# Chunk 0 of a fused retention and GELU-MLP kernel: two token units multiplied by seven half-size products, and a group of weight sums moved in VectorE's order

## The chip, the core and the metric

The kernel runs on one core of a Trainium2 chip. The core has a matrix engine (TensorE, "PE" in the profile, its weight loads "PEld"), a vector engine (VectorE, "DVE"), an engine for activations (ScalarE, "ACT"), GpSimd ("POOL"), which here issues the loads, and SyncE ("SP"), which issues the stores and the transposing transfers. Each engine takes its instructions in the order of the program and waits on semaphores for the others. The metric is the device time of one execution in microseconds; lower is better.

## What is computed

Eight heads of retention attention, without a softmax, over 8 sequences of 576 tokens, and then an MLP with a sigmoid-approximated GELU over all 4608 tokens:

```python
scores = scale * np.matmul(q, k.transpose(0, 1, 3, 2))
gamma = 1.0 - 2.0 ** (-5.0 - np.arange(H))
Dmat = np.where(rel >= 0, gamma[:, None, None] ** rel, 0.0)
attn_out = np.matmul(scores * Dmat, v)             # [8, 8, 576, 64]
x = attn_out.transpose(0, 2, 1, 3).reshape(4608, 512)
h = x @ w_in                                       # 512 x 2048
g = h * (1.0 / (1.0 + np.exp(-1.702 * h)))
out = g @ w_out                                    # 2048 x 512
```

## The kernel before

**Tiling.** The 4608 tokens are 36 units of 128 tokens (two units of four blocks of 64 for each pair of sequences, and one that joins their tails); four units make a chunk, so there are nine chunks. For each unit the kernel loads K, Q and V (`load`, on POOL's queue), transposes K and Q (`transposes` on PE with copies by DVE and ACT for the early units, `dma_transpose` on SP's queue from unit 8 on), scales V by powers of gamma (`scale_v`, L351, DVE), and then works in blocks of 64 tokens: masked scores inside a block (`scores`, `scores_out`), the running state K^T V (`state_both`, L427, on PE; `state_sum`, L440, on DVE; `state_cast`, L452, on ACT) and the products with both (`inter`, `values`), whose sum is scaled into xT (`x_out_pair`, L548, DVE). `block` strings these together for two units.

**The MLP.** For each of 16 slices f of the hidden width, `up` (L560) makes four matmuls of 128x512 over the chunk's 512 tokens and ACT's Gelu writes gT. The second product, g @ w_out, is made in one of two ways. `down` (L588) is the plain one: for one unit r and a group s of four slices, four matmuls of 128x512, 16 for a unit; `finish_unit` copies the bank out by ACT and stores it. `Pair` (L637) takes two groups of tokens at once by the Strassen-Winograd scheme: gT and w_out are each split in two along the hidden width (even and odd slices), tokens in two rows, the output in two column halves; instead of eight half-size products there are seven, with sums made beforehand and afterwards. The sums of gT are made by `Pair.sums` (L650): three additions into `gsum` and two subtractions in place. The sums of w_out are made once by `wsums` (L622), five operations for each of the four loaded groups of w_out. `Pair.run` (L696) makes the seven products in PSUM banks a and b by turns; three quarters are copied out by ACT (`copy`), six combinations go to DVE (`comb`). Between the products it calls `hook(i)`, where the caller puts other work. In `product` a matmul names the sum that it reads, so it waits for that one alone: `wsummed(n)` gives sum n of slices 2k and 2k+1 under the key of group k // 2.

**Order.** `Program.op` appends each operation to its engine's list in the order in which the Python code calls it, and derives waits from keys that it reads and writes. Nothing is reordered afterwards: an operation that waits holds up all that follows it on its engine.

**The stage of the change.** `lead_in` (L819) does units 0 to 7 up to their transposes and chunk 0's MLP. After `up(0, f)` for f = 8 to 15 (L912) come the second products of chunk 0, all by `down`: units 0 and 1 by turns (banks A and B) through s = 0 to 3, then unit 2, then unit 3. After each `down` of unit 1 a group of w_out sums is made. Six pieces of work for units 4 to 7 are put between the `down` calls, by the dictionary `work` with (unit, group) as key: the transposes and V scalings of units 4, 5, 6, 7, the scores and states of units 4 and 5 (`ahead45`), and their block (`block(2, ...)`). At (1, 3) the scaling of V of unit 4 and its transposes are called ahead of the last `wsums`. In chunks 1 to 7 (`steady`) all second products are made by `Pair(0, 2, 2)`, in chunk 8 units 3 and 0 by `Pair(3, 0, 1)` and units 1 and 2 by `down`.

**Banks.** PSUM banks C, D serve scores, K, E states, X, Y the block outputs, A and B the MLP; the transposes of early units borrow C, D, E, K and B. `turn()` gives A and B alternately.

Of the kernel before, what the change touches and what calls it, by code (L numbers as in the profile page):

```python
# [160 lines left out]
def bass_retnet_parallel__then__act_gelu_quick_kernel(  # L161
# [10 lines left out]
    with es:  # L172
# [160 lines left out]
        def gq_next(t):  # L333
            dst, src = gq[:, t, :, :], gq[:, 0, :, :]
            if t == 4:
                for i in range(2):
                    op("dve", lambda e, i=i: e.tensor_tensor(
                        gq[:, 4, :, 64 * i : 64 * i + 64], gq[:, 0, :, 0:64],
                        gpow[:, 4, :, None].to_broadcast([P, 4, 64]), ALU.mult),
                       reads=[f"gq{a}_0" for a in range(4)] + ["gpow4"], writes=[f"gq{a}_4" for a in range(4)])  # L340
                return
            if t == 5:
                op("dve", lambda e: e.tensor_copy(dst, src),
                   reads=[f"gq{a}_0" for a in range(4)], writes=[f"gq{a}_5" for a in range(4)])
                return
            op("dve", lambda e: e.tensor_tensor(
                dst, src, gpow[:, t, :, None].to_broadcast([P, 4, P]), ALU.mult),
               reads=[f"gq{a}_0" for a in range(4)] + [f"gpow{t}"], writes=[f"gq{a}_{t}" for a in range(4)])
# [211 lines left out]
        def up(c, f, lo=0, hi=4, b=None):  # L560
            b = b or "AB"[f % 2]
            n0, n1 = P * lo, P * hi
            for a in range(4):
                op("pe", lambda e, a=a: e.matmul(  # L564
                    bank[b][:, n0:n1], w_in_sb[:, a, P * f : P * f + P], xT[c % 2][:, a, n0:n1],
                    start=(a == 0), stop=(a == 3)),
                   reads=[f"win{f}"] + [f"x{c % 2}_{j}_{hh}" for j in range(lo, hi) for hh in range(2)],
                   writes=[b])
            op("act", lambda e: e.activation(  # L569
                gT[:, f, n0:n1], bank[b][:, n0:n1], AF.Gelu_apprx_sigmoid),  # L570
               reads=[b], writes=[f"g_{f}_{j}" for j in range(lo, hi)])
# [16 lines left out]
        def down(c, r, s, b, n0=0, n1=DM):  # L588
            for f in range(4 * s, 4 * s + 4):
                op("pe", lambda e, f=f: e.matmul(  # L590
                    bank[b][:, 0 : n1 - n0], gT[:, f, P * r : P * r + P], w_out_sb[:, f, n0:n1],
                    start=(f == 0), stop=(f == NF - 1)),
                   reads=[f"g_{f}_{r}", f"wout{f // 4}"], writes=[b])
# [42 lines left out]

        class Pair:  # L637

            def __init__(self, r0, r1, nt):
                self.r, self.nt, self.n = (r0, r1), nt, P * nt  # L640

            def gpart(self, row, col, f0, f1):
                t0 = P * self.r[row]
# [6 lines left out]
            def sums(self, f0, f1):  # L650
                a, g = (lambda r, c: self.gpart(r, c, f0, f1)), (lambda r, c: self.gkeys(r, c, f0, f1))
                for n, x, y in ((1, (1, 0), (1, 1)), (2, (0, 0), (0, 1)), (0, (0, 0), (1, 1))):
                    op("dve", lambda e, n=n, x=x, y=y: e.tensor_tensor(  # L653
                        gsum[:, n, f0 // 2 : f1 // 2, 0 : self.n], a(*x), a(*y), ALU.add),
                       reads=g(*x) + g(*y), writes=[f"gs{n}_{k}" for k in range(f0 // 2, f1 // 2)])
                for x, y in (((1, 0), (0, 0)), ((0, 1), (1, 1))):
                    op("dve", lambda e, x=x, y=y: e.tensor_tensor(a(*x), a(*x), a(*y), ALU.subtract),  # L657
                       reads=g(*x) + g(*y), writes=g(*x))
# [5 lines left out]
                return f  # L664

            def summed(self, n):
                return lambda k, t: (gsum[:, n, k, P * t : P * t + P], f"gs{n}_{k}")

            def product(self, b, left, right, more=False, late=0):

# [14 lines left out]
                return bank[b][:, 0 : 256 * self.nt].rearrange("p (t n) -> p t n", t=self.nt), [b]  # L685

            def tmp(self):
                return wtmp[:, 0 : 256 * self.nt].rearrange("p (t n) -> p t n", t=self.nt), ["wtmp"]

            def copy(self, dst, src):  # L690
                op("act", lambda e: e.activation(dst[0], src[0], AF.Copy), reads=src[1], writes=dst[1])  # L691
# [127 lines left out]
        def lead_in():  # L819
            load_kq0(0)  # L820
            load_kq0(1)
            iota_small()
            iota_large()
            load_v(0)
            load(1)
            load(2)
            load_win(0, 2)
            load_win(2, 2)
            load(3)
            load_win(4, 2)  # L830
            load_win(6, 2)
            load_win(8, 4)
            load_win(12, 4)
            for i in range(4):
                load_wout(i)
            for u in range(4, NPE + 4):
                load(u)
            op("dve", lambda e: e.memset(warmt.ap(), 0.0), writes=["warm"])
            warm_quads(NQUAD)
            warm(44, "A", 64)  # L840
            setup_dve()
            setup_dve2()
            setup_vfac()
            for a in range(4):
                gq_first(a)
            g_powers()
            gelu_table()
            cast_kq0(0, "dve")
            transpose_pe(0, 0, "E")
            transpose_copy(0, 0, "E", "dve")  # L850
            cast_kq0(1, "dve")
            warm(4)
            transpose_pe(0, 1, "B")
            transpose_copy(0, 1, "B", "dve")
            scale_v(0)
            warm(2)
            scores(0)
            scores_out(0, 1, 0)
            scores_out(0, 1, 1)
            warm(1, "A", 256)  # L860
            state_half(0, 0)
            transpose_pe(1, 0, "E")
            transpose_copy(1, 0, "E", "act")
            transpose_pe(1, 1, "B")
            transpose_copy(1, 1, "B", "act")
            scale_v(1)
            block1(0)
            warm(1, "A", 256)
            scores(1)
            scores_out(1, 1, 0)  # L870
            scores_out(1, 1, 1)
            gq_next(1)
            warm(1)
            state_half(1, 0)
            transpose_pe(2, 0, "E")
            transpose_copy(2, 0, "E", "act")
            warm(1)
            block1(1)
            transpose_pe(2, 1, "B")
            transpose_copy(2, 1, "B", "act")  # L880
            warm(2)
            scores(2)
            scale_v(2)
            scores_out(2, 1, 0)
            scores_out(2, 1, 1)
            up_group(0, 0, 2, 0, 2, "A")
            state_half(2, 0)
            up_group(0, 2, 2, 0, 2, "B")
            gq_next(2)
            block1(2)  # L890
            transpose_pe(3, 0, "E")
            transpose_copy(3, 0, "E", "dve")
            transpose_pe(3, 1, "D")
            transpose_copy(3, 1, "D", "act")
            up_group(0, 0, 4, 2, 3, "A")
            scale_v(3)
            scores(3)
            scores_out(3, 1, 0)
            scores_out(3, 1, 1)
            gq_next(3)  # L900
            warm(1, "E", 256)
            state_half(3, 0)
            up_group(0, 4, 2, 0, 2, "B")
            block1(3)
            up_group(0, 4, 2, 2, 3, "A")
            up_group(0, 6, 2, 0, 2, "B")
            up_group(0, 0, 4, 3, 4, "C")
            up_group(0, 4, 2, 3, 4, "A")
            up_group(0, 6, 2, 2, 4, "B")
            gq_next(4)  # L910
            gq_next(5)
            for f in range(8, NF):  # L912
                up(0, f)
            def ahead45():
                ahead(2)
                for u in (4, 5):
                    state_sum(u, 0)
                    state_sum(u, 1)
                state_cast(4, 6)
                scores_out(4, 2, 0)  # L920
                scores_out(4, 2, 1)

            work = {
                (1, 3): lambda: (scale_v(4), transposes(4, "E", "D", "dve")),
                (2, 0): lambda: (transposes(5, "E", "D", "dve"), scale_v(5)),
                (2, 1): ahead45,
                (3, 1): lambda: now(block(2, lambda: None)),
                (3, 2): lambda: (transposes(6, "C", "D", "dve"), scale_v(6)),
                (3, 3): lambda: (transposes(7, "E", "K", "dve"), scale_v(7)),
            }  # L930
            for r, s in [(i % 2, i // 2) for i in range(8)] + [(i // 4, i % 4) for i in range(8, NF)]:
                down(0, r, s, "AB"[r % 2])
                if (r, s) in work:
                    work[r, s]()
                if r == 1:
                    wsums(s)
                if s == 3:
                    finish_unit(0, r, "AB"[r % 2])

        def steady():  # L940
            four = Pair(0, 2, 2)
# [146 lines left out]
```

## Time and profile before

| | us |
|---|---|
| runs shown | 288.30, 289.47, 290.53 (median 289.47) |
| profiled execution | 289.72 |
| its span, first to last instruction | 287.9 |
| PE busy | 279.0 |
| DVE busy | 181.5 |
| ACT busy | 130.1 |
| POOL busy | 110.1 |

The mean granted clock of PE over the span is 0.994 of full speed. The chain that ended last is 82% PE, 7% POOL, 6% DMA and 3% DVE.

The profile is one execution. Times in it are microseconds from the start of the span. "L590" is line 590 of the kernel above. An instruction's row gives start, duration, engine, line, operation, the tile that it writes and those that it reads, their shapes, and in brackets how long the engine stood idle before it and which instruction of another engine released it. Rows of pipelined engines overlap a little, so a row of several (x5) is shorter than the sum of single durations.

### The profile page before, as it was taken

To read this page: it belongs to the slowest core of one execution; us is meant where nothing else is said; L and a number is where in the kernel's file an instruction comes from. 1 tells how busy PE (TensorE), PEld (TensorE's weight loads), DVE (VectorE), ACT (ScalarE), POOL (GpSimd) and SP (SyncE) were. 2 spreads that over 40 slices of the span, in tenths; PEclk is the share of its full clock that TensorE was granted. 3 is DMA by queue.
4 is the path that set the end of the run, shared out by engine and by line. 5 is a ranking of instruction groups with operands and counts; after the bars stand their busy time and mean duration, and the time that the engine had idled before them with its cause. 6 is when DMAs were issued, how large, how long until landed. Compare 5 with 4: busy or idle time off the path is not lost.

```text
span 287.9 us, 8938 instructions
## 1 busy us (share of the span) xinstructions
PE 279.0 (97%) x4010; PEld 178.7 (62%) x4010; DVE 181.5 (63%) x350; ACT 130.1 (45%) x229; POOL 110.1 (38%) x141
## 2 busy tenths in 40 slices
PE   8999999999879999999999999999999999999996
PEld 6575455888653488348834883488348834883474
DVE  5953667568857967495949593859395928650240
ACT  7456334662117541654175417531754175306611
POOL 9999889000870860068006900670072000000000
PEclk9999999999979999999999999999999999999999
DMA  9999999999999990889398978892896070012012
GB/s 171 180 205 206 202 234 249 235 142 202 101 234 243 104 194 21 229 99 198 68 224 105 171 99 233 111 181 73 227 114 74 13 208 2 2 64 84 0 55 93
DMA packets 116790, 40.69 MB, mean 141 GB/s; under 512 B 104080, under 2 KB 109968, under 8 KB 116752
## 3 DMA queue, kind: packets, MB, share of 16 engines
q0 software_dynamic: 79712, 22.82, 68.7%
q1 hardware_dynamic: 36896, 17.24, 23.0%
q8 instruction: 31, 0.51, 0.7%
q10 hardware_dynamic: 144, 0.07, 0.1%
q14 instruction: 7, 0.06, 0.1%
HBM read 36.70 MB, written 9.44 MB: 160 GB/s over the span
## 4 chain that ended last, share of the span: by engine, by line
PE 82%; POOL 7%; DMA 6%; DVE 3%; ACT 1%; issue 0%; POOLq 0%
PE psA L564 17%; PE psB L564 17%; PE psA L675 16%; PE psB L675 15%; DMA vn<-in_v_dram 6%; POOL w_in_sb L269 3%; PE psB L578 3%; PE psA L578 2%; PE psA L590 2%; PE psB L590 2%; POOL kqn L234 2%; PE psX L489 2%; POOL vn L247 1%; POOL w_out_sb L276 1%; PE psC L505 1%; PE psK L434 1%
## 5 line engine op out<-in xcount | busy, mean ns | idle before, releaser
L234 POOL DMA_DIRECT2D kqn<-in_k_dram x39 | 35.0, 907 | 106.1 <-DMA kqT<-kqn 104.4
L564 PE MATMUL psA<-xT,w_in_sb 128*128 128x512 bf16 x240 | 61.7, 379 | 0.0
L564 PE MATMUL psB<-xT,w_in_sb 128*128 128x512 bf16 x240 | 61.7, 379 | 0.0
L653 DVE TENSOR_TENSOR gsum<-gT 128x1024 bf16<-128x1024 bf16 (+1 forms) x48 | 28.7, 654 | 48.3 <-ACT gT L569 45.6
L569 ACT ACTIVATE gT<-psB 128x512 bf16<-128x512 f32 x60 | 35.8, 597 | 28.6 <-PE psB L564 28.4
L569 ACT ACTIVATE gT<-psA 128x512 bf16<-128x512 f32 x60 | 35.8, 597 | 22.5 <-PE psA L564 22.3
L564 PEld LDWEIGHTS psB<-xT,w_in_sb 128*128 128x128 bf16 x240 | 19.7, 97 | 31.2 <-ACT gT L569 14.2
L564 PEld LDWEIGHTS psA<-xT,w_in_sb 128*128 128x128 bf16 x240 | 19.4, 97 | 30.9 <-ACT gT L569 14.3
L247 POOL DMA_DIRECT2D vn<-in_v_dram x40 | 37.0, 939 | 0.1
L234 POOL DMA_DIRECT2D kqn<-in_q_dram x37 | 33.4, 915 | 0.6 <-issue 0.6
L675 PE MATMUL psA<-wsum,gT 128*128 128x256 bf16 x240 | 29.8, 278 | 0.0
L458 ACT ACTIVATE kv<-stm 128x1024 bf16<-128x1024 f32 (+1 forms) x18 | 15.5, 863 | 29.9 <-DVE stm L449 29.9
L675 PE MATMUL psB<-wsum,gT 128*128 128x256 bf16 x240 | 28.9, 273 | 0.0
L675 PEld LDWEIGHTS psA<-wsum,gT 128*128 128x128 bf16 x240 | 23.6, 100 | 4.2 <-ACT gT L569 1.0
L675 PEld LDWEIGHTS psB<-wsum,gT 128*128 128x128 bf16 x240 | 23.1, 98 | 4.1 <-ACT gT L569 1.5
L353 DVE TENSOR_TENSOR vp<-vn,vfac 128x512 bf16<-128x512 f32 x36 | 23.0, 684 | 3.5 <-DMA vn<-in_v_dram 3.5
L552 DVE TENSOR_TENSOR xT<-psX,gq 128x512 bf16<-128x512 f32 x16 | 11.0, 689 | 18.3 <-PE psX L527 18.3
L657 DVE TENSOR_TENSOR gT<-gT 128x1024 bf16<-128x1024 bf16 (+1 forms) x32 | 19.5, 651 | 0.0
L691 ACT ACTIVATE osb<-psA 128x512 f32<-128x512 f32 (+1 forms) x12 | 7.0, 579 | 23.1 <-PE psA L675 23.1
L691 ACT ACTIVATE osb<-psB 128x512 f32<-128x512 f32 (+1 forms) x12 | 6.7, 562 | 19.1 <-PE psB L675 19.1
L675 PE MATMUL psA<-w_out_sb,gsum 128*128 128x256 bf16 x120 | 14.6, 273 | 0.4 <-issue 0.3
L675 PE MATMUL psB<-w_out_sb,gsum 128*128 128x256 bf16 x120 | 14.4, 273 | 0.0
(108 smaller groups left out, 433.9 us busy)
## 6 DMA issues: line engine op xcount, KB each, us to landing
vn<-in_v_dram POOLq DMA_DIRECT2D x32, 256.0 KB, 4.9
out_dram<-osb SPq DMA_DIRECT2D x31, 256.0 KB, 2.3
kqn<-in_k_dram POOLq DMA_DIRECT2D x31, 128.0 KB, 4.6
kqn<-in_q_dram POOLq DMA_DIRECT2D x31, 128.0 KB, 5.0
w_out_sb<-in_moe_w_out_dram POOLq DMA_DIRECT2D x4, 512.0 KB, 13.4
w_in_sb<-in_moe_w_in_dram POOLq DMA_DIRECT2D x8, 128.0 KB, 5.3
w_in_sb<-in_moe_w_in_dram POOLq DMA_DIRECT2D x4, 256.0 KB, 7.5
vn<-in_v_dram POOLq DMA_DIRECT2D x8, 128.0 KB, 4.2
```

The costliest lines, as they stand in the source:

```text
L234: e.dma_start(kqn[sl][p0 : p0 + n, which, :, :], src[b, :, s0 : s0 + n, :].rearrange("h p d -> p h d"),)
L247: e.dma_start(vn[sl][p0 : p0 + n, :, :], v[b, :, s0 : s0 + n, :].rearrange("h p d -> p h d"))
L353: op(eng, lambda e: e.tensor_tensor(vp[u % NVP].ap(), vn[sl].ap(), vfac[:, ty, :, None].to_broadcast([P, H, DH]), ALU.mult), reads=[f"vn{s ...
L458: op("act", lambda e: e.activation(kv[:, i0 % NKV : i0 % NKV + n, :, :], stm[:, i0 % 8 : i0 % 8 + n, :, :], AF.Copy), reads=[f"stm{(i0 + i ...
L564: op("pe", lambda e, a=a: e.matmul(bank[b][:, n0:n1], w_in_sb[:, a, P * f : P * f + P], xT[c % 2][:, a, n0:n1], start=(a == 0), stop=(a == ...
L569: op("act", lambda e: e.activation(gT[:, f, n0:n1], bank[b][:, n0:n1], AF.Gelu_apprx_sigmoid), reads=[b], writes=[f"g_{f}_{j}" for j in ra ...
L578: op("pe", lambda e, a=a, f=f, i=i: e.matmul(bank[b][:, n * i : n * i + n], w_in_sb[:, a, P * f : P * f + P], xT[c % 2][:, a, P * lo : P * ...
L590: op("pe", lambda e, f=f: e.matmul(bank[b][:, 0 : n1 - n0], gT[:, f, P * r : P * r + P], w_out_sb[:, f, n0:n1], start=(f == 0), stop=(f == ...
L653: op("dve", lambda e, n=n, x=x, y=y: e.tensor_tensor(gsum[:, n, f0 // 2 : f1 // 2, 0 : self.n], a(*x), a(*y), ALU.add), reads=g(*x) + g(*y ...
L657: op("dve", lambda e, x=x, y=y: e.tensor_tensor(a(*x), a(*x), a(*y), ALU.subtract), reads=g(*x) + g(*y), writes=g(*x))
L675: op("pe", lambda e, x=x, y=y, t=t, s=not more and t == 0 and k == 0, z=k == NF // 2 - 1: e.matmul(bank[b][:, 256 * t : 256 * t + 256], x, ...
L691: op("act", lambda e: e.activation(dst[0], src[0], AF.Copy), reads=src[1], writes=dst[1])
```

## The change

Three things are changed.

`Pair` takes a fourth argument `at`, the place in `gsum` and `wtmp` where its sums and its intermediate result lie, and the keys of these become one for each 128 columns.

In chunk 0 units 2 and 3 are multiplied by `Pair(2, 3, 1).run` instead of by eight calls of `down`. Their sums are called in two halves, `sums(0, 8)` ahead of `up(0, 8)` and `sums(8, 16)` after the last `up`, both ahead of the loop that calls `wsums`. The pieces of work that stood after the `down` calls of units 2 and 3 go into the hooks of the run in the same order (hook 0 for (2, 0), and so on to hook 6 for (3, 2)); the piece of (3, 3) follows the run. Units 2 and 3 are then stored in the order 3, 2.

In the loop over units 0 and 1, `wsums(s)` is called ahead of the piece of work and no longer after it. Since only (1, 3) has one there, the last group of w_out sums comes ahead of unit 4's scaling of V and of its transposes' copies.

`Pair.run` calls `turn()` three times, so that banks A and B change places in the chunks that follow.

```diff
-            def __init__(self, r0, r1, nt):
-                self.r, self.nt, self.n = (r0, r1), nt, P * nt
+            def __init__(self, r0, r1, nt, at=0):
+
+                self.r, self.nt, self.n, self.at = (r0, r1), nt, P * nt, P * at
+
+            def places(self):
+                return range(self.at // P, self.at // P + self.nt)
...
-                        gsum[:, n, f0 // 2 : f1 // 2, 0 : self.n], a(*x), a(*y), ALU.add),
-                       reads=g(*x) + g(*y), writes=[f"gs{n}_{k}" for k in range(f0 // 2, f1 // 2)])
+                        gsum[:, n, f0 // 2 : f1 // 2, self.at : self.at + self.n], a(*x), a(*y), ALU.add),
+                       reads=g(*x) + g(*y), writes=[f"gs{n}_{k}_{j}" for j in self.places() for k in range(f0 // 2, f1 // 2)])
...
             def tmp(self):
-                return wtmp[:, 0 : 256 * self.nt].rearrange("p (t n) -> p t n", t=self.nt), ["wtmp"]
+                w = wtmp[:, 2 * self.at : 2 * self.at + 256 * self.nt]
+                return w.rearrange("p (t n) -> p t n", t=self.nt), [f"wtmp{j}" for j in self.places()]
...
             gq_next(4)
             gq_next(5)
+            pair = Pair(2, 3, 1)
+            pair.sums(0, 8)
             for f in range(8, NF):
                 up(0, f)
+            pair.sums(8, 16)
...
-            for r, s in [(i % 2, i // 2) for i in range(8)] + [(i // 4, i % 4) for i in range(8, NF)]:
-                down(0, r, s, "AB"[r % 2])
+            for i in range(8):
+                r, s = i % 2, i // 2
+                down(0, r, s, "AB"[r])
+                if r == 1:
+                    wsums(s)
                 if (r, s) in work:
                     work[r, s]()
-                if r == 1:
-                    wsums(s)
                 if s == 3:
-                    finish_unit(0, r, "AB"[r % 2])
+                    finish_unit(0, r, "AB"[r])
+
+            def hook(i):
+                k = (2 + i // 4, i % 4)
+                if k in work:
+                    work[k]()
+
+            pair.run(0, hook)
+            work[3, 3]()
```

More of the change, by code (lines that the diff above doesn't have):

```diff
@@ L666, in summed @@
             def summed(self, n):
-                return lambda k, t: (gsum[:, n, k, P * t : P * t + P], f"gs{n}_{k}")
+                return lambda k, t: (gsum[:, n, k, self.at + P * t : self.at + P * t + P], f"gs{n}_{k}_{self.at // P + t}")
             def product(self, b, left, right, more=False, late=0):
```

## The prediction

> **What bounds the kernel now.** I read the page first, for the engine that is full and for the clock.
>
> ```profile
> PE 279.0 (97%) x4010; PEld 178.7 (62%) x4010; DVE 181.5 (63%) x350; ACT 130.1 (45%) x229; POOL 110.1 (38%) x141
> ...
> PEclk9999999999979999999999999999999999999999
> ```
>
> TensorE (PE) is busy 279.0 of 287.9 us: fewer columns on it would help, if it is never made to wait instead. One slice has a lower clock. The change lies near 24 to 54 us, so I next listed VectorE (DVE) there in order of time (start, duration, engine, line, operation, count, idle time before it and what ended that).
>
> ```profile
> 22.34 0.97 DVE L343 COPY gq<-gq 128x512 f32<-128x512 f32 x1
> 27.84 1.77 DVE L630 TENSOR_TENSOR wsum<-w_out_sb 128x512 bf16<-128x512 bf16 x5 [4.53 <-DMA w_out_sb<-in_moe_w_out_dram]
> 30.53 1.77 DVE L630 TENSOR_TENSOR wsum<-w_out_sb 128x512 bf16<-128x512 bf16 x5 [0.92 <-DMA w_out_sb<-in_moe_w_out_dram]
> 33.13 1.77 DVE L630 TENSOR_TENSOR wsum<-w_out_sb 128x512 bf16<-128x512 bf16 x5 [0.83 <-DMA w_out_sb<-in_moe_w_out_dram]
> 38.10 0.69 DVE L353 TENSOR_TENSOR vp<-vn,vfac 128x512 bf16<-128x512 f32 x1 [3.21 <-DMA vn<-in_v_dram]
> 38.71 0.42 DVE L385 COPY kqT<-psE 128x512 bf16<-128x512 bf16 x1
> 39.05 1.76 DVE L630 TENSOR_TENSOR wsum<-w_out_sb 128x512 bf16<-128x512 bf16 x5
> 40.72 0.42 DVE L385 COPY kqT<-psE 128x512 bf16<-128x512 bf16 x1
> 41.05 0.68 DVE L353 TENSOR_TENSOR vp<-vn,vfac 128x512 bf16<-128x512 f32 x1
> ```
>
> Three of the four groups of w_out sums are made in time that DVE has free while w_out arrives; the fourth stands behind unit 4's scaling, which waits for V until 38.10. Nobody on PE reads these sums before 65 us now. Then ACT and the chain of waits around the same stage and at the end:
>
> ```profile
> 31.53 0.60 ACT L569 ACTIVATE gT<-psB 128x512 bf16<-128x512 f32 x1 [0.27 <-PE psB L564]
> 44.05 1.06 ACT L458 ACTIVATE kv<-stm 128x1024 bf16<-128x1024 f32 x1 [3.21 <-DVE stm L449]
> 45.02 0.58 ACT L611 ACTIVATE osb<-psA 128x512 f32<-128x512 f32 x1
> ```
>
> ```profile
> 274.86 1.05 PE psA L675 x8
> 275.91 0.87 PE psB L675 x8
> ```
>
> The last Gelu of chunk 0 ends at 31.53 + 0.60 = 32.13. The state cast starts 2.01 us after PE ended the state products (42.04), and ACT is free for the next at 45.02, 2.98 us after them. The last two lines are from the chain: a seven-product run over one unit pair exists already in the last chunk, 0.87 us for each product of eight 128x256 matmuls, 1.05 for one that starts after a wait. Last, PE's own waits and the clock in 1 us windows (length, PE busy, count, clock, DMA share, GB/s):
>
> ```profile
> 73.97 0.21 PE L489 MATMUL psX<-kqT,kv 64*64 64x64 bf16 x1 [0.96 <-ACT kv L458]
> ...
> 81.30 0.21 PE L489 MATMUL psX<-kqT,kv 64*64 64x64 bf16 x1 [2.51 <-ACT kv L458]
> ```
>
> ```profile
> 80.00:81.00 1.00, 0.00 (x0) 1.00 1.76 226
> 81.00:82.00 1.00, 0.70 (x64) 0.78 1.62 250
> 82.00:83.00 1.00, 1.00 (x78) 0.50 1.64 249
> ...
> 85.00:86.00 1.00, 1.00 (x10) 1.00 2.24 172
> ```
>
> A wait of 2.51 us halved the clock: 0.78 in the slice from 81 is 0.44 us at half speed, so it ran from 81.56 to 85, some 3.4 us. A wait of 0.96 us left it at 1.00.
>
> **The gain on PE.** Units 2 and 3 now cost eight groups of four 128x512 matmuls, 0.86 us each; they become seven products of 0.87. That is 6.9 - 6.1 = 0.8 us less.
>
> **The cost on DVE.** The sums of units 2 and 3 are two times five operations on 128x512. The nearest row, the w_out sums, has 0.42 us each and 1.68 us for five in a row. The first five need Gelus that end by 25.2 (24.62 + 0.60) and lie in the idle time from 23.3 to 27.84: nothing. The second five need the last Gelu, so they start at 32.2 and end at 33.85. They stand ahead of all w_out sums in DVE's order, so DVE idles where it made three groups before, and what is queued behind them is late: w_out sums 33.85 + 4 x 1.68 = 40.57, unit 4's scaling (0.61) to 41.2, its key transpose copy out of bank E to 41.6. Putting the last group ahead of the scaling removes the wait for V, but not this: V is there at 38.08.
>
> **PE, step by step.** PE reaches the new run at 38.68, as now (the eight groups of units 0 and 1 and unit 4's transposes do not read the sums).
> Product 0 reads the fifth w_out sum of every group. Its first six matmuls need groups 0 to 2 (38.98) and end at 39.34; the last two need group 3, at 40.66. Stall 1.37 us. With 0.2 for a start after a wait (1.05 - 0.87) it ends at 41.1.
> Unit 5's transposes reuse bank E, free at 41.6. Stall 0.55; they end at 42.2.
> Product 1 ends at 43.05, the scores and states of units 4 and 5 at 43.95 (0.88, as now without its 0.15 wait).
> Products 2 and 3 end at 45.7. Product 4 writes bank A, which ScalarE (ACT) must first copy out after product 2, and that copy is queued behind the state cast, which waits for the four state sums. ACT is free 2.98 after 43.95, at 46.93; the copy is 0.38 (the last chunk's rows, 384 ns); PE goes on at 47.35. Stall 1.65. Now the same cast costs PE only some 0.1, ahead of unit 4's inter-block products.
> Products 4 and 5 (1.05 + 0.87), units 4 and 5's block (0.84, from 45.67 to 46.51 now), product 6 (0.87) and the transposes of units 6 and 7 (0.88) end at 51.85. Now that point is at 49.24: 2.6 later.
> Next is DVE once more: from 50.2 two x copies (1.2), the last combination (0.34), two transpose copies (0.67) and two V scalings (1.22) end at 53.6. The states of unit 7 wait for that and end near 53.85, 50.75 now. So 3.1 later; with the 0.2 for the starts taken as nothing, 2.9. I take 3.0.
>
> **What costs nothing.** Six combinations of 128x256 (0.42 each) lie in DVE's waits for PE and ACT, apart from the one counted above. ACT loses two copies of 0.6 and gains three of 0.38. The stores of units 3 and 2 come some 1.5 us later on SP, and the six transposes behind them start at 62.44 now, after V of unit 13, so 11 us cover them. Nothing on POOL's queue is moved. Banks A and B change places in all later chunks; both have the same rows. The finer keys of the sums order the same pairs of operations. From 53.9 on PE waits only for work that hangs on PE itself (the two waits shown), so a delay stays to the end; 288 us hold no other wait to take it up.
>
> **The sum.** Profiled execution: 287.9 + 3.0 = 290.9 us of span, and 1.8 around it, 292.7. It lies 0.25 over the median of the three runs, so from 289.47 the forecast is 292.5.
>
> **The clock.** My gaps of 1.37 and 0.55 lie within 2.3 us, with 0.4 of work between them, and a third of 1.65 follows 4 us later. They lie between the row that kept the clock (0.96) and the one that lost it (2.51). If it falls as at 81.5, half of 3.4 us is lost, 1.7; some of that runs in the stall before product 4, so the price is 0 to 1.7. I take none, as no gap is as long as 2.51, and keep 1.7 for the range.
> [...]
>
> **Rivals.**
> Faster than before: DVE's sums are not late for PE. Then the gain alone is left, 289.47 - 0.8 = 288.7. It holds if the w_out sums end before 38.7, that is, if the four groups take under 4.8 us from 33.85 instead of 6.7. For it: DVE is only 63% busy. Against it: 1.77 in all four rows. 9%.
> The clock falls too: all stalls, plus about 1.1 for half speed: 293.6, up to 294.2. For it the row at 81.3; against it that each gap is shorter. 23%.
> The delay is taken up: chunk 1's waits of 0.96 and 2.51 end by something that is timed by the loads, not by PE, and shrink by what PE is late. Then 289.5 to 291, by how much of the 3.0 goes there. The rows name ACT's cast after DVE's sums after PE, which speaks against it; a wait is put down to its last releaser only. 12%.
> The half-clock stretch of 81.5 to 85 is not met this time, as other work falls around it: 292.5 - 1.7 = 290.8. 6%.
> The change says seven products and has seven, so that it does not do what it says is no case.
>
> **How the numbers follow.** My case, three stalls at full clock, has 50%: 292.5, its own range 291.4 to 293.5 (half a microsecond of working, and the 2.2 us between the three runs shown). The range for 8 in 10 reaches down to the cases of partial cover, 290.0, and up through the lower clock, 294.3. A change of 1%, 2.9 us, is about what this measurement tells from none. My case lies just over that bound: I give 0.27 of its 0.50 to slower, with 0.22 of the lower clock's 0.23 and 0.04 of the rest: 0.53. Faster by over 1% (under 286.6) needs the rival without stalls and the better clock together: 0.04. The rest, 0.43, is within 1%.
>
> **What would show it.** In the changed profile: the second set of gT sums near 32.2 and the w_out sums in one block from 33.9 to 40.6; a PE wait of about 1.4 for wsum inside the first product, one of about 0.5 for bank E, one of about 1.6 for ACT's osb copy behind the kv cast; the first Gelu groups of chunk 1 some 2.6 later; 81.3 moved to about 84.3. I am wrong if the w_out sums end before 39, if product 4 starts without waiting for ACT, or if the waits of chunk 1 are shorter than 0.96 and 2.51.

## The result, and the profile after

| | kernel before | changed kernel |
|---|---|---|
| median of 6 runs each | 290.09 us | 293.90 us |
| range of the runs | 288.30 to 291.07 | 292.37 to 296.41 |
| ratio, 95% interval | | 1.014 [1.0093, 1.0186] |
| span of the profiled execution | 287.9 | 294.3 |

The changed kernel is slower. The profiled execution is 6.4 us longer than the one of before, more than the medians differ, so I first took it apart. VectorE's rows in order of time (start, duration, engine, line, operation, count, idle time before and what ended it):

```profile
27.12 1.10 DVE L657 TENSOR_TENSOR gsum<-gT 128x512 bf16<-128x512 bf16 x3 [2.06 <-ACT gT L583]
28.14 0.75 DVE L661 TENSOR_TENSOR gT<-gT 128x512 bf16<-128x512 bf16 x2
34.03 1.10 DVE L657 TENSOR_TENSOR gsum<-gT 128x512 bf16<-128x512 bf16 x3 [5.14 <-ACT gT L569]
35.04 0.75 DVE L661 TENSOR_TENSOR gT<-gT 128x512 bf16<-128x512 bf16 x2
35.72 6.79 DVE L630 TENSOR_TENSOR wsum<-w_out_sb 128x512 bf16<-128x512 bf16 x20
42.42 0.68 DVE L353 TENSOR_TENSOR vp<-vn,vfac 128x512 bf16<-128x512 f32 x1
```

Where the kernel before made three groups of w_out sums while they arrived, DVE now stands 5.14 us for the last Gelu and then makes all twenty sums in one block of 6.79 us. PE: the first row of product 0, the rows that wait, and the second Gelu groups of chunk 1 (55.58):

```profile
40.55 0.82 PE L679 MATMUL psA<-wsum,gT 128*128 128x256 bf16 x6
42.56 0.39 PE L679 MATMUL psA<-wsum,gT 128*128 128x256 bf16 x2 [1.19 <-DVE wsum L630]
43.50 0.40 PE L369 MATMUL psE<-ident,kqn 128*128 128x128 bf16 x4 [0.55 <-DVE kqT L385]
...
48.97 1.05 PE L679 MATMUL psA<-wsum,gsum 128*128 128x256 bf16 x8 [1.48 <-ACT osb L696]
...
55.58 1.05 PE L578 MATMUL psA<-xT,w_in_sb 128*128 128x256 bf16 x8
```

In the kernel before the same two points are these (its first group of unit 2, and its second Gelu groups of chunk 1):

```profile
38.68 1.03 PE L590 MATMUL psA<-w_out_sb,gT 128*128 128x512 bf16 x4
...
50.68 1.05 PE L578 MATMUL psB<-xT,w_in_sb 128*128 128x256 bf16 x8
```

From one to the other PE needs 15.03 us now and needed 12.00, which is 3.03 more. I call this the stage below. Two more differences lie outside of it, both rows of PE in the changed kernel:

```profile
15.81 1.89 PE L578 MATMUL psB<-xT,w_in_sb 128*128 128x256 bf16 x8 [1.71 <-DMA w_in_sb<-in_moe_w_in_dram]
...
200.79 1.47 PE L679 MATMUL psA<-w_out_sb,gsum 128*128 128x256 bf16 x12 [1.50 <-issue]
```

At 15.81 PE had waited 1.71 us for w_in, ahead of everything that the change touches, and from 15.8 to 19.2 its clock was granted at 0.50 only; so the stage begins at 40.55 instead of 38.68, 1.87 later. At 199 us it stopped for 1.50 us, between two matmuls of one product, for nothing that the profile shows ("issue"). 1.87 + 3.03 + 1.50 is the 6.4 us. Whether the first and the third belong to the change was the first question for the experiments.

### The profile page after: what moved, and what is told of

Read it like the earlier page. It is cut to its first block, busy times and chain, and to the rows that moved or that the text cites. A ratio compares the mean times of both kernels' runs of the same rounds, so it can differ in the third digit from the quotient of the medians.

```text
span 294.3 us, 9006 instructions
## 1 busy us (share of the span) xinstructions
PE 279.9 (95%) x4034; PEld 181.5 (62%) x4034; DVE 186.8 (63%) x366; ACT 130.1 (44%) x230; POOL 110.1 (37%) x141
## 4 chain that ended last, share of the span: by engine, by line
PE 85%; DVE 6%; POOL 3%; DMA 2%; ACT 2%; issue 1%; POOLq 0%; DVEq 0%
PE psB L564 18%; PE psA L564 18%; PE psB L679 17%; PE psA L679 15%; PE psB L578 4%; PE psA L578 3%; DVE wsum L630 2%; DMA w_in_sb<-in_moe_w_in_dram 2%; PE psX L489 2%; PE psB L590 1%; PE psC L505 1%; POOL vn L247 1%; PE psY L527 1%; PE psX L527 1%; ACT kv L458 1%
## 5 line engine op out<-in xcount | busy, mean ns | idle before, releaser
L657 DVE TENSOR_TENSOR gsum<-gT 128x1024 bf16<-128x1024 bf16 (+1 forms) x54 | 30.9, 628 | 55.7 <-ACT gT L569 50.9
L679 PE MATMUL psB<-wsum,gT 128*128 128x256 bf16 x256 | 32.5, 281 | 0.0
L679 PE MATMUL psA<-wsum,gT 128*128 128x256 bf16 x256 | 31.2, 273 | 1.2 <-DVE wsum L630 1.2
L679 PEld LDWEIGHTS psB<-wsum,gT 128*128 128x128 bf16 x256 | 25.4, 101 | 4.5 <-ACT gT L569 1.0
L679 PEld LDWEIGHTS psA<-wsum,gT 128*128 128x128 bf16 x256 | 24.5, 98 | 5.7 <-ACT gT L569 1.5
L661 DVE TENSOR_TENSOR gT<-gT 128x1024 bf16<-128x1024 bf16 (+1 forms) x36 | 21.0, 624 | 0.0
L696 ACT ACTIVATE osb<-psB 128x512 f32<-128x512 f32 (+1 forms) x13 | 7.3, 564 | 22.7 <-PE psB L679 22.7
L679 PE MATMUL psA<-w_out_sb,gsum 128*128 128x256 bf16 x128 | 15.6, 273 | 1.5 <-issue 1.5
L679 PE MATMUL psB<-w_out_sb,gsum 128*128 128x256 bf16 x128 | 15.5, 273 | 0.1
```

Source lines behind the costliest of these rows:

```text
L657: op("dve", lambda e, n=n, x=x, y=y: e.tensor_tensor(gsum[:, n, f0 // 2 : f1 // 2, self.at : self.at + self.n], a(*x), a(*y), ALU.add), re ...
L679: op("pe", lambda e, x=x, y=y, t=t, s=not more and t == 0 and k == 0, z=k == NF // 2 - 1: e.matmul(bank[b][:, 256 * t : 256 * t + 256], x, ...
```

## The experiments

Each kernel was timed 6 or 12 times beside the kernel before, except one that ran once. The stage is read from each kernel's own profile, from the first matmul of product 0 (or of unit 2's first group) to the first of the second Gelu groups of chunk 1. "Stops" are PE's waits without a releaser of 0.4 us and more after 24 us.

| kernel | ratio to before, 95% interval | stage, us | stops, us |
|---|---|---|---|
| before | | 12.00 | none |
| changed, first time | 1.014 [1.0093, 1.0186] | 15.03 | 1.5 |
| changed, again | 1.0084 [1.0054, 1.0115] | 15.02 | none (one of 0.38) |
| gT sums between the w_out sums | 1.0027 [0.9995, 1.0058] | 13.25 | none |
| state cast behind the copies | 1.0124 [1.009, 1.0159] | 15.04 | 1.5, 1.0 |
| both | 1.0057 [1.0026, 1.0087] | 14.27 | 1.6, 0.9 |
| both, V of units 6 and 7 early | 1.0032 [1.0001, 1.0064] | 12.45 | 1.1, 0.4, 0.4 |
| only the move, on the kernel before | 1.0012 [0.998, 1.0045] | 12.26 | none |
| changed, the move undone | 1.0127 [1.0082, 1.0171] | 16.06 | 0.9, 0.6 |
| before, products of units 2 and 3 halved | 1.0095 [1.0064, 1.0125] | 13.48 | 0.7, 0.6, 1.4 |
| block behind product 6 | 1.0053 [1.0024, 1.0081] | 13.65 | 0.9 |
| shifted by 64 instructions (one run) | | 12.28 | 0.7 |
| block split round product 6 | 1.0037 [1.0006, 1.0069] | 12.53 | 0.7 |
| all that helped, together | 1.0012 [0.9987, 1.0037] | 11.41 | 0.7 |

My theory was that the three waits shown above make the loss. The rivals were that the seven products and their combinations are dear in themselves, and that the lead-in is what got longer.

**The changed kernel again.**

> The changed kernel once more, beside the others of this call. In its first profile three things lie over the kernel before: 1.9 us ahead of 40 us, where PE waited 1.71 us for w_in, 3.0 us in the changed stage, and 1.5 us at 199 us, where PE waited for nothing that the profile shows. Theory of the three waits: only the 3.0 belong to the change, +2.5 to +3.5 us against before (1.009 to 1.012), and the wait for w_in and the one at 199 us are absent or of another size this time. Rival 'the lead-in is what got longer': PE waits over 1.5 us for w_in again, and the ratio is 1.014 or more.

1.0084 [1.0054, 1.0115]; the medians are 293.04 and 290.36, 2.7 us apart. The stage is 15.02 us again, with the same 1.19, 0.55 and 1.49. No wait of PE for w_in of 0.3 us or more is in this profile and the stop near 199 us is 0.38, at 196.03. So the wait for w_in is chance, and of the first profile's excess only the stage comes back in full.

**The sums of gT called later.**

```diff
-            pair.sums(8, 16)
             def ahead45():
...
                 if r == 1:
                     wsums(s)
+                    if s == 2:
+                        pair.sums(8, 16)
```

> The second set of gT sums is called after the third group of w_out sums instead of ahead of the first. Theory of the three waits (the changed kernel loses 1.2 to 1.4 us to the late w_out sums, 0.55 to bank E and 1.5 to the osb copy behind the state cast): the first two waits go, the third stays. DVE makes the first three groups of w_out sums at 27.8 to 34.9, the gT sums to 36.6, the fourth group to 38.3. So some 2.1 us under the changed kernel, +0.9 us against the kernel before (ratio 1.003). Rival 'the seven products and their combinations are dear in themselves, wherever the sums stand': the time stays at that of the changed kernel, +3 to +4 us (1.010 to 1.014). Rival 'the lead-in is what got longer': the same, +3 to +4, with a longer wait for w_in ahead of 20 us.

1.0027 [0.9995, 1.0058], the stage 13.25. PE's rows:

```profile
38.68 1.04 PE L679 MATMUL psA<-wsum,gT 128*128 128x256 bf16 x8
...
45.32 1.05 PE L679 MATMUL psA<-wsum,gsum 128*128 128x256 bf16 x8 [1.48 <-ACT osb L696]
...
51.93 1.05 PE L578 MATMUL psA<-xT,w_in_sb 128*128 128x256 bf16 x8
```

All eight matmuls of product 0 run in one piece, and the stage is 1.8 us shorter. DVE's order was 1.8 of the 3.0 us, as the theory said; called where DVE has time, the sums make PE wait nowhere.

**The state cast called later.**

```diff
-                state_cast(4, 6)
                 scores_out(4, 2, 0)
...
+                (2, 3): lambda: state_cast(4, 6),
                 (3, 1): lambda: now(block(2, lambda: None)),
```

> The state cast of units 4 and 5 on ACT is called after the copy that follows product 3 and no longer ahead of the copy that follows product 2; the sums stay late. Theory of the three waits: the waits for w_out sums (1.2) and bank E (0.55) stay, product 4 no longer waits (1.5 gone) and the block of units 4 and 5 waits for the cast by at most 0.2. So some 1.5 us under the changed kernel, +1.5 us against before (1.005). Rival 'dear in themselves': no change from the changed kernel (1.010 to 1.014). Rival within the theory, that the block merely waits in product 4's place: the wait moves to the inter-block products and the time stays, 1.010 or more.

This is a miss: 1.0124 [1.009, 1.0159], the stage 15.04 and so no shorter at all. Product 4 no longer waits, but another wait has taken its place, and not the block's for the cast, which was my rival. PE stops inside that block, and the profile names no releaser:

```profile
50.35 0.22 PE L527 MATMUL psY<-pm,vp 64*64 64x64 bf16 x2 [1.49 <-issue]
```

**Both edits.**

> Both edits together: sums between the third and fourth group of w_out sums, and the state cast behind the copies. Theory of the three waits: no PE wait over 0.3 us is left between 31 and 49 us, what is left is the gain of one group of matmuls (0.8) less 0.5 for the late scaling of unit 7's V, plus the 0.3 of small waits that the kernel before had: -0.3 to -0.9 us against before (0.997 to 0.999). Rival 'dear in themselves': still over before, +2 or more (1.007).

A miss again, 1.0057 [1.0026, 1.0087] where I expected less than 1. PE in this kernel, inside the block of units 4 and 5, and the instruction queue's line for 47.2 to 48.4 us (transfers, MB, share of 16 engines' time):

```profile
49.83 0.22 PE L527 MATMUL psY<-pm,vp 64*64 64x64 bf16 x2 [1.64 <-issue]
```

```profile
q8 instruction: 1, 0.02, 5.3%
```

PE stops for 1.64 us among the second value products. Their scores had been masked by 46.92, their tiles are in place, and the instructions just before them on the same operands had run; the profile names no releaser. One transfer of the instruction queue lies there, from 47.35 to 48.37; PE goes on 1.5 us after it. In the version with early V (below) the transfer ends at 46.24 and PE goes on at 47.55, 1.3 later. The whole run has 31 such transfers with 0.51 MB, 16 KB each, and PE's 4034 weight loads, with a matmul each (4014 of these are recorded), are nearly all of the program's instructions. So I formed a second theory: PE uses up its instructions faster than they come. Half-size matmuls need twice as many for the same columns, and they lie between two dense stretches, the scores and states (over 60 small matmuls in 0.9 us) and the block (some 60 in 0.84 us). In the traces of the kernel before and of the changed one a transfer starts for every 127.5 and 127.1 weight loads on the mean, from the first of the 31 to the last. So one carries some 255 of PE's instructions, about 64 bytes each; that is an estimate from these counts. The spacing of the stops agrees with it (last section); how much of this PE holds at a time isn't shown by any run here.

**V of units 6 and 7 early.** As both edits, with `scale_v(6)` called after product 3 and `scale_v(7)` after product 4.

> As the one with both edits, and the scalings of V of units 6 and 7 are called after products 3 and 4 instead of after the transposes that follow the run. Theory: the last lateness of DVE at the start of chunk 1 (0.5 us, states of unit 7 waiting for V) goes too: -1.0 to -1.4 us against before (0.995 to 0.997), 0.5 under the version with both edits. If V of units 6 or 7 has not landed by then (it is called for at 27 and 30 us and takes some 15), DVE waits for it and the gain is lost. Rival 'dear in themselves': over before.

1.0032 [1.0001, 1.0064]; the wait at the start of chunk 1 is gone, the stop of 1.10 at 47.55 stays, and the stage is 12.45. Less the stop it would be 11.35, under the 12.00 of before; that is a sum, not a run.

**Halving without anything else.** The test of the second theory on the kernel before, with no sums, no combinations and no moved call:

```diff
+                for n in (0, 256):
+                    op("pe", lambda e, f=f, n=n: e.matmul(
+                        bank[b][:, n : n + 256], gT[:, f, P * r : P * r + P], w_out_sb[:, f, n : n + 256],
...
-                down(0, r, s, "AB"[r % 2])
+                (down if r < 2 else down_halves)(0, r, s, "AB"[r % 2])
```

> The kernel before, with the products of units 2 and 3 of chunk 0 made by twice as many matmuls of 128x256 in place of 128x512: the same columns, no sums, no combinations, the same copies. It asks what stopped PE for 1.1 to 1.6 us inside the block of units 4 and 5 in the versions with the cast moved, in a place where no semaphore is waited for, 1.3 to 1.5 us after a 16 KB transfer of instructions. Theory 'PE runs out of instructions, as half-size matmuls use them up at twice the rate': here too PE stops for 0.5 to 1.6 us without a releaser near 46 to 48 us, +0.5 to +1.6 us (1.002 to 1.005). Rival 'that stop belongs to the sums, the combinations or the moved cast': no such stop, ratio 1.000.

1.0095 [1.0064, 1.0125], more than I expected, and in two places of its profile near the stage:

```profile
47.47 0.21 PE L527 MATMUL psY<-pm,vp 64*64 64x64 bf16 x1 [0.73 <-issue]
...
54.34 0.27 PE L578 MATMUL psA<-xT,w_in_sb 128*128 128x256 bf16 x1 [0.62 <-issue]
```

A third stop, 1.43 us, lies at 196.00 us. The three are 2.8 us together, and the medians are 2.3 apart. The stage of 13.48 holds only the first of them; some 0.5 of its excess lies where PE waits 0.25 us for the queries of unit 5 to land, and the run of only the move, below, has that wait too. The columns are the same, and a group of eight half-size matmuls takes the 0.87 us of four whole ones; the stops come with the additional instructions alone. So half of the rival "dear in themselves" holds: not the products' time and not the combinations, but their number of instructions. The stop stands at the block where both versions with the moved cast have theirs.

**Only the move, and the move undone.** The second part of the change alone, put on the kernel before, and the changed kernel without it:

```diff
+                if r == 1:
+                    wsums(s)
                 if (r, s) in work:
                     work[r, s]()
-                if r == 1:
-                    wsums(s)
```

> The kernel before with only the order of the last w_out sums and unit 4's scaling changed. The sums then end by 37.5 in the time in which DVE waits for V, unit 4's scaling starts at 38.1 as now, and unit 5's key copy and scaling come some 0.7 us sooner, so that PE's small waits at 41 and 41.8 us (0.15 to 0.4) go: 0 to -0.4 us, 0.9985 to 1.000, which is hardly to be told from none. A rival for the loss of the changed kernel, that this move delays unit 4, would show +1 us or more (1.003).

1.0012 [0.998, 1.0045]: the move alone does nothing that can be told from none. PE's small wait at 41.8 us is gone, but it now waits 0.24 us for the queries of unit 5 to land, and the stage is 12.26.

> The changed kernel with its second part undone: unit 4's scaling and key copy stand ahead of the last w_out sums again. By the rows of the changed kernel DVE then makes groups 0 to 2 of the w_out sums until some 39.0 (counted from a lead-in as in the kernel before), scales unit 4 to 39.6, copies to 40.0, and makes the last group to 41.6. So bank E is free in time (0.55 gone), and the wait for w_out sums grows from 1.19 to 2.1; the wait for the osb copy stays. Theory of the three waits: +0.3 to +0.5 us against the changed kernel, so 1.010 to 1.012 against before. Rival 'the move itself costs': under the changed kernel (1.006 or less).

1.0127 [1.0082, 1.0171]. Its wait for the sums, and the clock in 1 us windows after it (length, PE busy, count, clock, DMA share, GB/s):

```profile
41.48 0.39 PE L679 MATMUL psA<-wsum,gT 128*128 128x256 bf16 x2 [2.12 <-DVE wsum L630]
```

```profile
42.00:43.00 1.00, 1.00 (x12) 0.78 1.37 303
43.00:44.00 1.00, 1.00 (x34) 0.50 2.17 225
44.00:45.00 1.00, 1.00 (x55) 0.50 1.26 327
45.00:46.00 1.00, 1.00 (x6) 0.51 1.93 214
```

The wait is 2.12, as expected, and bank E no longer holds PE up. In this profile the clock also fell to 0.50 after it, so that the stage, 16.06, is longer than the waits alone would make it. With the changed kernel at 1.0084 to 1.014, the timing doesn't show what the move is worth in it; the rows do: it turns a wait of 2.12 into 1.19 and 0.55.

**Where the block stands.** Two attempts to put product 6 where PE stops.

> As the version with both edits and the early scalings of V, and the block of units 4 and 5 is called after product 6 instead of before it. If PE runs out of instructions there because the dense block comes too soon after the dense scores and states, 0.87 us of product 6 now lies between: the stop without a releaser shrinks from 1.1 to 0.2 or so, but the first Gelu groups of chunk 1 wait some 0.4 for the x copies: -0.4 us against that version, about 0 against before (0.999 to 1.002). Rival: the stop is tied to its place in the instruction stream and keeps its 1.1 us, 1.003 or more.

A miss, 1.0053 [1.0024, 1.0081]. The stop in the block is gone, as the theory has it, but product 6 now waits:

```profile
47.19 1.05 PE L679 MATMUL psA<-wsum,gT 128*128 128x256 bf16 x8 [1.18 <-DVE osb L699]
```

The combination that frees bank A stands on DVE near the early scaling of unit 7, and that waited 0.88 us for V; I had priced V's landing for the version before and forgotten it here.

> Both edits, V of units 6 and 7 scaled after product 4 and after the first half of the block, and the block of units 4 and 5 split round product 6: its inter-block products and first value products before, the second value products after it. By the running-out theory 0.87 us of product 6 lie where PE stopped for 1.1, so 0.3 of the stop is left; the x copies end at 49.2, where chunk 1 could start at 48.7. So second Gelu groups of chunk 1 some 12.1 to 12.3 us after product 0, where the kernel before needs 12.0 and the version with early V 12.45: 1.000 to 1.002. A version over both kernels is not expected. Rival, that the stop keeps its 1.1 us: 12.9 or more.

1.0037 [1.0006, 1.0069], the stage 12.53 and not 12.1 to 12.3. In the block a wait is left that the profile puts down to PE's own product 6:

```profile
48.01 0.22 PE L527 MATMUL psY<-pm,vp 64*64 64x64 bf16 x2 [0.43 <-PE psA L679]
```

It lies at the same weight load as the stops in this block, and 1.34 us after a transfer of instructions, so I read it as the rest of the stop, for which 0.3 was expected. The x copies make PE wait another 0.43, and a stop of 0.67 is at 54.73, after the stage.

**Shifted instructions.** The version with early V, with `NQUAD` 25 instead of 57: 32 of the warming matmuls ahead of all work are left out, so that all later PE instructions come 64 places earlier in the stream, a quarter of the some 255 that one transfer carries by the estimate above.

> The version with both edits and early V, with 32 small warming matmuls fewer at the very start (64 fewer PE instructions with their weight loads), so that all later PE instructions stand 64 places earlier in the stream. If what stops PE without a releaser is the end of a fetched piece of 256 instructions (16 KB of 64 bytes), the stop moves by 64 PE instructions to later ones, out of the block, to product 6 or the transposes after it; its length may change. If it belongs to the block of units 4 and 5 itself (its switch of tile size, its banks), it stays at the same instruction of the block, 1.1 to 1.6 us.

One run: 289.27 us, beside 290.00 for the median of 17 runs of the kernel before, which a single run can't tell apart. The profile has the answer:

```profile
56.45 0.19 PE L489 MATMUL psY<-kqT,kv 64*64 64x64 bf16 x1 [0.66 <-issue]
```

Nothing stops in the block of units 4 and 5; the stop, 0.66 now, is in the next one, of units 6 and 7. The same instructions that stopped PE for 1.10 run through when only their place in the stream has changed, so the block itself isn't the cause. The place of the old stop did move nearly as expected: counted in weight loads it is now the first Gelu group of chunk 1, at 49.28, just behind the transposes. But PE gets there 2.37 us after the transfer's end and waits for the x copies, not for instructions. The stop at 56.45 is at the next such place, which I had not expected; the last section has the count.

**All that helped.**

```diff
-NQUAD = 57
+NQUAD = 25
...
-            pair.sums(8, 16)
...
-                state_cast(4, 6)
...
+                (2, 3): lambda: state_cast(4, 6),
+                (3, 0): lambda: scale_v(6),
                 (3, 1): lambda: now(block(2, lambda: None)),
-                (3, 2): lambda: (transposes(6, "C", "D", "dve"), scale_v(6)),
+                (3, 2): lambda: transposes(6, "C", "D", "dve"),
...
                     wsums(s)
+                    if s == 2:
+                        pair.sums(8, 16)
```

> What the runs point to, put together: the sums between the third and fourth group of w_out sums, the state cast behind the copies, 32 warming matmuls fewer at the start, V of unit 6 scaled after product 4 and V of unit 7 after the transposes that follow the run. In the shifted version no stop without a releaser lay in the block of units 4 and 5, one of 0.66 us lay in the block of units 6 and 7 at 56 us, and PE waited 0.33 for the DVE combination ahead of product 6 and 0.49 for the x copies. The later scaling of unit 7 takes the 0.33 away and some of the 0.49. So the second Gelu groups of chunk 1 come 11.7 to 12.0 us after product 0 (12.0 in the kernel before), and the stop of 0.7 at 56 us stays: 0 to +0.5 us against before, 0.999 to 1.002. Only if that stop goes too is it faster, by 0.3 to 0.8 us (0.997).

1.0012 [0.9987, 1.0037]. Its PE rows at the ends of the stage:

```profile
38.58 1.04 PE L679 MATMUL psA<-wsum,gT 128*128 128x256 bf16 x8
...
49.99 1.05 PE L578 MATMUL psA<-xT,w_in_sb 128*128 128x256 bf16 x8
```

The stage takes 11.41 us, 0.6 less than in the kernel before and less than I expected: here the gain of the seven products is seen on PE. A stop of 0.67 without a releaser in the block of units 6 and 7 (55.57) takes it back: from 0.69 us ahead of the kernel before, PE is 0.16 behind at the next Gelu group. At 69.27 it waits 0.20 for a transposing transfer, and is 0.54 behind from there. The time is that of the kernel before. No version faster than the kernel before was found; how the stops could be had out of the whole program was not tried further.

## Why the prediction held, and where it did not

The forecast was 292.5 us in a range of 290.0 to 294.3, slower by 3.0; measured are 293.9 and, the second time, 293.04 us, 3.8 and 2.7 over the kernel before.

**The gain on PE** was right as a term: 0.8 was said, and 0.6 is left in the stage where no wait covers it.

**DVE.** Less the 1.87 us of the lead-in, the second gT sums start at 32.16 (32.2 was said), the w_out sums at 33.85 (33.85), unit 4's scaling at 40.55 (40.57). Durations from the rows of before carried over to a few hundredths, since the same operations were only put in another order.

**PE's waits.** 1.37 was said for the w_out sums (its two times, 40.66 and 39.34, are only 1.32 apart), 1.19 is the row; 0.55 for bank E, 0.55; 1.65 for the copy behind the cast, 1.48. The first Gelu groups of chunk 1 come 2.5 later (2.6 was said: 53.45 less 1.87, against 49.08), the second ones 3.03 (2.9 to 3.1). That a delay stays to the end holds too: the state casts of chunk 1 stood at 80.19 and 89.92 before and stand at 85.08 and 94.98 now, 4.89 and 5.06 later, of which 1.87 is the lead-in.

**The clock.** It stayed at 1.00 through the stage in both profiles of the changed kernel, so taking none of the 1.7 was right there. But I had argued it from the length of the gaps, and in other versions a stop of 1.64 and a wait of 2.12 us were followed by half clock: see below. So the reason given was not the right one, and that the clock held here is in part luck.

**The rivals.** "DVE's sums are not late for PE" fell by the 1.19 row. "The delay is taken up by chunk 1's waits" fell: they are 0.95 and 2.5 as before. "The half-clock stretch is not met" came true in 5 of the 12 later runs of the changed kernel, whose mean clock is 1.000, and in 10 of the 35 runs of the kernel before beside them, so it is no effect of the change.

**How near.** The 2.7 us of the later runs are the better test of the 3.0, since the lead-in has no such wait there. The first median lies 0.4 under the end of the range; of that profile's 6.4 us, 1.87 (the lead-in) and 1.50 (the stop) stood in no term of the sum.

**What the sum left out.** The products were counted by their time alone, "seven products of 0.87". That is true, but they are 24 matmuls and 24 weight loads more, and the supply of instructions was no term of the sum. In the stage of the changed kernel this cost is just hidden. Its transfer of instructions starts at 49.04, when product 4 has started after its wait (48.97), and PE reaches the place where the others stop at 51.49, 1.46 us after the transfer's end. With the cast moved, the transfer starts at 47.92, PE is there at 48.66, and goes on at 50.35, again 1.46 us after the end. So taking the wait for ACT's copy away leaves the stage as it is (15.03 and 15.04). Where the place lies elsewhere, the wait is worth what was said: from the version with only the sums moved to the last one, the first Gelu groups of chunk 1 come 1.54 us sooner after product 0 (11.11 and 9.57); these two differ in V of unit 6 and the 32 warming matmuls as well. In the rest of the program the cost shows: 1.50 and 0.38 us near 199 us.

## What to carry to other kernels

When work is put on an engine that is idle on the average, look at what stands behind it in that engine's order and when its inputs come: five operations that wait for the last Gelu cost 1.8 of the three microseconds, because twenty others stood behind them, fifteen of which had been free. When a wait is predicted, ask what is late next if it goes, and test it by taking it away. And count instructions as well as columns: where matmuls were halved next to stretches of many small ones, PE stopped for 0.4 to 1.6 us at a time, for want of instructions by the reading of these runs, and the profile shows it as a wait without a releaser, 1.2 to 1.7 us after a transfer of the instruction queue. A change far ahead in the program moved such a stop (32 matmuls fewer at the start: 1.10 us in the block of units 4 and 5, then 0.66 in that of units 6 and 7), so a version should not be judged by one of them.

## What the runs showed of the hardware

**Stops for instructions.** The two profiled kernels with the old number of PE instructions show no stop without a releaser of 0.4 us or more after 24 us; of the twelve profiles of kernels with halved products, ten do, from 0.7 to 2.8 us in sum, an eleventh has one of 0.38, and the twelfth (the sums called later) has none. Counting PE's weight loads from the start, each with one matmul behind it, says where they lie. The count stands after the x, up to just before PE goes on: early V, the halving (two stops), the shift, and the changed kernel (length, PEld busy, count, clock, DMA share, GB/s):

```profile
0.00:47.54 47.54, 28.33 (x731) 1.00 1.45 202
0.00:47.46 47.46, 29.02 (x731) 1.00 1.46 204
0.00:54.33 54.33, 34.41 (x858) 1.00 1.52 208
0.00:56.44 56.44, 35.15 (x858) 1.00 1.50 209
0.00:200.78 200.78, 125.33 (x3031) 0.98 1.17 168
```

All 17 stops, and the one of 0.38 with them, lie behind load 731 (four), 858 (four), 2647 or 2648 (two) or 3031 (eight), whatever operation stands there: in kernels with different orders of work, and in two with 32 loads left out ahead. From one place to the next it is 127, 1789 or 1790, and 383 or 384 loads, near 1, 14 and 3 times 128; from the start of one transfer to the next it is 127.5 on the mean in the kernel before. And in all of them PE goes on 1.2 to 1.7 us after the end of a 16 KB transfer of the instruction queue. So that PE runs out of instructions there rests on three things: the halving alone, the shift, and this count. What sets the start of a transfer, and what PE does in the 1.2 to 1.7 us behind its end, wasn't found. In the kernel before, a transfer lies from 45.22 to 46.19 and stops nobody: PE gets to load 731 only 2.4 us after its end.

**The clock does not follow the length of a gap.** The wait of 2.5 us in chunk 1 is in all profiles, and in the kernel before it was followed by 3.4 us of half clock. In the changed kernel's second profile and in four others (the sums called later, the cast called later, the halving, the shift) the mean clock over the whole span is 1.000, so there it was not. With both edits a stop of 1.64 us was followed by over 3 us of half clock, which makes that version's stage longer than the stop:

```profile
50.00:51.00 1.00, 1.00 (x15) 0.72 2.04 222
51.00:52.00 1.00, 1.00 (x10) 0.50 2.08 228
52.00:53.00 1.00, 1.00 (x12) 0.50 1.47 292
53.00:54.00 1.00, 1.00 (x9) 0.58 1.82 246
```

In the changed kernel's first profile it fell after the 1.71 us wait for w_in and once more after the 2.51:

```profile
15.00:16.00 1.00, 0.19 (x2) 0.88 1.50 276
19.00:20.00 1.00, 1.00 (x16) 0.91 1.26 203
87.00:88.00 1.00, 1.00 (x53) 0.72 1.51 287
```

Worked out as in the prediction, these two falls start at 15.76 and 87.44, 71.7 us apart, and each lasts 3.4 us. With both edits there are two as well, at 16.30 and 50.44, 34.1 apart. That is 21.0 and 10.0 times 3.41 us. The 3.41 is the length of the fall in the kernel before, where the clock is 0.50 from 81.56 to 84.97. That falls start whole multiples of it apart is an estimate from these two pairs alone; what decides whether a gap is followed by a fall isn't shown by any run here.

Of the 17 runs of the kernel before that stood beside the shifted one, 14 have a mean clock of 0.994 and three of 1.000. So whether a gap costs this is chance from one execution to the next, up to 1.7 us here by the prediction's reckoning of 3.4 us at half clock; beside the later runs of the changed kernel, the runs of the kernel before with 0.994 have a median 1.25 us over those with 1.000. The clock also favours the version with the sums called later, whose ratio of 1.0027 has 7 of 12 runs at 1.000 against 6 of 29 of the kernel before: among runs of the same mean clock it is 1.8 (0.994) and 1.2 us (1.000) slower, which fits its stage better.

**The lead-in is chance too.** PE's wait for w_in near 14 to 16 us was 0.38 in the kernel before, 1.71 in the first profile of the changed one and under 0.3 in its second, with the same instructions up to there.
